# One w2 fetch moved up, weight sums spread over rounds, balancing in two parts, a sum of x in halves: attention and eight routed experts on one Trainium2 core

## The chip, the cores and the metric

The kernel runs on one core of one Trainium2 chip. The core has five engines that run side by side, each with its own queue of instructions that it works through strictly in order: TensorE (matmuls, PE in the profile; its weight loads are PEld), VectorE (DVE), ScalarE (ACT), GpSimd (POOL) and SyncE (SP). Engines wait for each other through semaphores. Matmuls write to PSUM, a small memory of eight banks of 128 x 512 float32 values, which VectorE and ScalarE empty into the larger SBUF. GpSimd's queue also issues the DMA transfers that bring in weights. The metric is the device time of one execution in microseconds, taken as the median of several runs; less is better.

## The reference

Attention over 4 x 8 heads with 768 positions of 64 features: an 8 x 8 matrix per head is balanced (five times exp, rows divided by their sums, columns divided by theirs) and mixes blocks of 96 keys and values before an ordinary softmax attention. Its output is x, 3072 tokens of 512 features, the input of eight experts:

```python
logits = x @ w_gate
logits = logits - logits.max()
P = np.exp(logits)
for _ in range(8):
    P /= P.sum(1, keepdims=True) + 1e-09
    P /= P.sum(0, keepdims=True) + 1e-09
    P *= N / E
for e in range(E):
    h = np.maximum(x @ w1[e], 0.0)
    ye = h @ w2[e]
    out += P[:, e:e + 1] * ye
```

Every token goes through every expert (512 to 1024 hidden features and back to 512), and the 3072 x 8 weights P come out of eight balancing iterations over the whole table.

## The kernel before

**Stages.** Up to about 125 us the kernel does the attention, batch by batch, with expert 0 for the tokens that are done between its matmuls. From there on it does the last tokens of expert 0 (the generator `last_dense`, lines 765 and 773), the eight balancing iterations (the generator `balance`), and experts 1 to 7.

**Experts 1 to 7** multiply in Strassen's way: seven products of quarter matrices instead of eight, paid for with sums. Four kinds of sums are needed: of w1 (`sum_w`, line 406, eight additions for an expert, GpSimd), of w2 (`sum_w2`, line 518, eight, GpSimd), of x (`sum_x`, line 528, four for each third of the tokens; one third on VectorE before the stage, one on GpSimd, and the last, `sum_x(2)`, on VectorE), and of the hidden values (`Pair.sums`, line 691, three on GpSimd for each pair of token tiles, into a tile `hs`; line 641 on GpSimd or line 644 on VectorE for one more, `s3`). Sums of w1 and the fourth sum of x are in place.

**Rounds.** The main loop runs over rounds r. A chunk n is one third of the tokens (p) of one expert (e) and takes four rounds (i = 0 to 3). In each round there are seven steps p1, p5, p6, p2, p7, p3, p4 (`hidden`, matmuls at line 590) of the chunk, and between them seven products q1 to q7 (line 701) of the pair k = r - 5, in the order q5, q7 of the pair before, q1, q4 of the pair before, q6, q2, q3. In the rounds 0 to 4 there is no pair yet, and what is left of `last_dense` stands between the steps. PSUM has a ring of five banks `bk` for the steps and of three banks `oacc` for the products; the third of these holds the balancing's table until round 5.

After p7 and p3 VectorE evicts a bank with line 579 (relu of a sum, into the hidden values hT); after p2 and p4 ScalarE does it with line 576. After a product VectorE adds the weighted result to the output (`gather`, line 651). q1 goes to the same bank as q5, and waits for the gather of q5.

**The order of the work** is written out by hand: every instruction of this stage is pinned, so each engine gets its instructions in the order in which the Python code calls them.

- GpSimd in a round: the load of w1 or w2 if one is due (lines 89 and 94), then the three sums of the pair of the next round, then `weights(n)`, which takes n sums from a queue of generators. A load is a DMA that GpSimd issues; the sums that read it wait for its landing on GpSimd, and with them all that is queued behind. Expert 2's w2 is loaded in round 8, and the queue gets its sums there; `weights` takes 4 in the rounds 5, 6 and 7, and then 1 or 2 in turn:

```python
weights((0, 2, 2, 0, 0)[r] if r < 5 else 4 if r < 8 else 1 + i % 2)
```

- The balancing generator is advanced by `next(chain)`: seven times between the steps of `last_dense`, by the letters C of a string, and in the rounds 0 to 4 after three of every four steps. An iteration has three parts: row sums and their reciprocals (lines 560 to 562, VectorE); the division by them and the column sums over the tiles (lines 564 and 565); then one small matmul over the partitions (line 567, TensorE), its reciprocal and the division (lines 568 to 571, VectorE). The matmul is in TensorE's queue like any other, and all that is behind it waits until VectorE's column sums are there.

- The four sums of `sum_x(2)` are advanced by the letters X of the same string (three), and the last of them, in place on xtT, at the end of round 6. Round 8 is the first to read it.

Of the kernel before, what the change touches and what calls it, by code (L numbers as in the profile page):

```python
# [17 lines left out]
ALU = mybir.AluOpType  # L18


def mkap(t, dims, off=0):
    return bass.AP(tensor=t.tensor, offset=t.offset + off, ap=dims)
# [3 lines left out]
def kernel(  # L26
# [14 lines left out]
    N, Dm, E, F = 3072, 512, 8, 1024  # L41
# [45 lines left out]
    def load_w1(e):  # L87
        w1t[e] = wp.tile([128, 4, F], BF16, name="w1e")
        pin(nc.gpsimd.dma_start(out=w1t[e],
                                in_=moe_w1[e].rearrange("(kk k) f -> k kk f", k=128)))  # L90

    def load_w2(e):
        w2t[e] = (wq if e else wcp).tile([128, 8, Dm], BF16, name="w2e")
        pin(nc.gpsimd.dma_start(out=w2t[e],
                                in_=moe_w2[e].rearrange("(fb k) f -> k fb f", k=128)))
# [302 lines left out]
    def sum_w(e):  # L398
        wct[e] = (wcq if e % 2 == 0 else wcp).tile([128, 3, 2, F // 2], BF16, name="wc")
        for kk in range(2):  # L400
            a11, a21 = (w1t[e][:, kk, f:f + 512] for f in (0, 512))
            a12, a22 = (w1t[e][:, 2 + kk, f:f + 512] for f in (0, 512))
            s1, s2, s4 = (wct[e][:, j, kk, :] for j in range(3))
            for a, b, o, c in ((a21, a22, ALU.add, s1), (s1, a11, ALU.subtract, s2),
                               (a11, a21, ALU.subtract, a21), (a12, s2, ALU.subtract, s4)):
                pin(nc.gpsimd.tensor_tensor(out=c, in0=a, in1=b, op=o))  # L406
                yield

    with tc.tile_pool(name="ps0", bufs=7, space=bass.MemoryType.PSUM,
# [37 lines left out]
        for h in range(0, 8, 2):  # L447
            nc.vector.tensor_tensor(
                out=Rt[0][:, h:h + 2],
                in0=mkap(pbps, [pbps.ap[0], [1, 2], [32, 8], [0, 16]], off=h),  # L450
                in1=mkap(mask16, [mask16.ap[0], [0, 2], [0, 8], [1, 16]]), op=ALU.mult)
# [71 lines left out]
    def sum_x(p, eng, hold=pin):  # L523
        ta, tb = (slice(1024 * p + 512 * i, 1024 * p + 512 * i + 512) for i in range(2))
        b11, b12, b21, b22 = (xtT[:, k:k + 2, t] for k in (0, 2) for t in (ta, tb))
        x1, x2, x4 = (xc[:, j, :, 512 * p:512 * p + 512] for j in range(3))
        for a, b, c in ((b12, b11, x1), (b22, x1, x2), (b21, x2, x4), (b22, b12, b12)):
            hold(eng.tensor_tensor(out=c, in0=a, in1=b, op=ALU.subtract))
            yield

    onesc = mpc.tile([128, 128], F32)
    nc.gpsimd.memset(onesc, 1.0)
# [2 lines left out]
    for _ in sum_x(0, nc.vector, lambda ins: ins):  # L535
        pass

    def balance():

        room = rings["oacc"][2]  # L540
        G = room[:, 0:NT * E].rearrange("p (t e) -> p t e", e=E)
        sums = room[:, 192:192 + NT]
        csps = room[:, 256:256 + E]
        gmps = room[:, 384:512]
        gm = mpc.tile([128, 1], F32)
        pin(nc.vector.reduce_max(out=gm, in_=glog.rearrange("p t e -> p (t e)"), axis=AX.X))
        pin(nc.tensor.matmul(gmps[0:1, :], gm, I128, start=True, stop=True))
        gm1 = mpc.tile([1, 1], F32)
        pin(nc.vector.reduce_max(out=gm1, in_=gmps[0:1, :], axis=AX.X, negate=True))
        yield  # L550
        pin(nc.tensor.matmul(csps[:, 0:1], onesc[0:1, :], gm1, start=True, stop=True))
        gneg = mpc.tile([128, 1], F32)
        pin(nc.vector.tensor_copy(gneg, csps[:, 0:1]))
        pin(nc.scalar.activation(out=G, in_=glog, func=AF.Exp, bias=gneg))
        rs2 = mpc.tile([128, NT], F32)
        cs2 = mpc.tile([128, E], F32)
        cs1 = mpc.tile([128, E], F32)
        yield
        for it in range(8):
            pin(nc.vector.reduce_sum(out=sums, in_=G, axis=AX.X))  # L560
            pin(nc.vector.tensor_scalar_add(rs2, sums, 1e-9))
            pin(nc.vector.reciprocal(out=rs2, in_=rs2))
            yield
            pin(nc.vector.tensor_mul(G, G, mkap(rs2, [rs2.ap[0], rs2.ap[1], [0, E]])))
            pin(nc.vector.reduce_sum(out=cs2, in_=G.rearrange("p t e -> p e t"), axis=AX.X))
            yield
            pin(nc.tensor.matmul(csps, onesc, cs2, start=True, stop=True))
            pin(nc.vector.tensor_scalar(out=cs1, in0=csps, scalar1=float(E) / N,
                                        scalar2=1e-9 * E / N, op0=ALU.mult, op1=ALU.add))
            pin(nc.vector.reciprocal(out=cs1, in_=cs1))  # L570
            pin(nc.vector.tensor_mul(glog if it == 7 else G, G,
                                     mkap(cs1, [cs1.ap[0], [0, NT], cs1.ap[1]])))
            yield
# [168 lines left out]
    def scale0(ts):  # L742
        for t in ts:
            pin(nc.scalar.activation(out=osbl[:, t, :], in_=osbl[:, t, :], func=AF.Copy,
                                     scale=glog[:, t, 0:1]))

    def last_dense():
# [7 lines left out]
        for c in range(2):  # L755
# [14 lines left out]
            for tt in range(3):  # L770
# [7 lines left out]
                yield  # L778

    dense, chain, xs = last_dense(), balance(), sum_x(2, nc.vector)  # L780
    for step in "TTCXTTCXTTCCXTTCCTTTCTT":
        next({"T": dense, "C": chain, "X": xs}[step])
    held_x = mpc.tile([128, 2], BF16)
    pin(nc.gpsimd.tensor_copy(held_x, xc[:, 2, 0, 1024:1026]))

    queue = [sum_w2(1), sum_x(1, nc.gpsimd)]

    def weights(n):
        while n and queue:
            if next(queue[0], 0) is None:  # L790
                n -= 1
            else:
                queue.pop(0)
# [7 lines left out]
    for m, o in enumerate(ends):  # L801
        e, p, hT, _ = chunks[-1]
# [4 lines left out]
    for r in range(len(pairs) + 6):  # L807
        n, i = r // 4, r % 4
        if n < C:
            e, p, hT, s3 = chunks[n]  # L810
            if i == 0 and (n == 1 or n > 1 and p == 0) and e + 1 < E:
                load_w1(e + 1)
                queue.append(sum_w(e + 1))
            if r == 8 or p == 1 and i == 2 and n > 1 and e + 1 < E:
                load_w2(2 if r == 8 else e + 1)
                queue.append(sum_w2(2 if r == 8 else e + 1))
            steps, rest = hidden(e, p, i, hT, s3, r < 4)
        else:
            steps, spares, rest = spares[:7], spares[7:], None
        k = r - 5  # L820
        if k + 1 in range(len(pairs)):
            pairs[k + 1].sums()
        weights((0, 2, 2, 0, 0)[r] if r < 5 else 4 if r < 8 else 1 + i % 2)
        now = pairs[k] if k in range(len(pairs)) else None
        if r < 5:
            outs = [lambda: next(dense), None, lambda: next(dense), None,
                    lambda: next(dense)]
        else:
            outs = [getattr(a, b) for a, b in
                    ((now, "q5"), (before, "q7"), (now, "q1"), (before, "q4"),  # L830
                     (now, "q6"), (now, "q2"), (now, "q3")) if a]
        if now and now.last:
            plains, steps = iter(steps), []
            outs = [next(plains) if o == "x" else getattr(before if o[1:] else now, "q" + o[0])
                    for o in "5 7' x 1 x 4' 6 x 2 x 7 x x 3 4".split()]
            now = None
        if r == 5:
            for _ in chain:
                pass
        for j in range(max(len(steps), len(outs))):  # L840
            if j < len(steps):
                steps[j]()
                if j == 3 and n < C:
                    if k + 1 in range(1, 12):
                        scale0([8 * ((k + 1) // 4) + (k + 1) % 4 + 4 * m for m in range(2)])
                    if k + 1 in range(len(pairs)):
                        pairs[k + 1].keep()
            if j < len(outs) and outs[j]:
                outs[j]()
            if r < 5 and j != 3 and (6 * r + j - (j > 3)) % 4 != 3:  # L850
                next(chain, 0)
            if r == 4 and j in (2, 5):
                scale0([4 if j == 2 else 0])
            if j == 1 and late:
                late()
                late = None
            if r == 6 and j == 6:
                next(xs)
        late, before = rest, now
        if n >= C and not spares and not before:  # L860
            break
# [30 lines left out]
```

## Time and profile before

| what | us |
|---|---|
| median of 3 runs | 669.74 (669.25 to 670.33) |
| the profiled execution | 669.11 |
| its span, first to last instruction | 667.3 |
| TensorE busy | 653.6 |
| VectorE busy | 475.2 |
| GpSimd busy | 470.8 |
| ScalarE busy | 386.3 |
| TensorE's granted clock | 1.00 throughout |

The profile comes from one execution. "Busy" is the time in which an engine had an instruction under way. A list of waits names an engine, the instruction that waited, and the one that released it, with the total in us, the number of times and the longest. A view in order of time gives the start in us, the duration of an instruction or of several alike in a row (xN), the engine, the line in the code, the operation, and output and inputs with their shapes; in brackets, when the engine stood idle before it, for how long and who released it. Matmuls overlap, so a group's duration reaches beyond the start of the next. GpSimd's starts and ends are rougher than those of the others.

### The profile page before, as it was taken

To read this page: it belongs to the slowest core of one execution; us is meant where nothing else is said; L and a number is where in the kernel's file an instruction comes from. 1 tells how busy PE (TensorE), PEld (TensorE's weight loads), DVE (VectorE), ACT (ScalarE), POOL (GpSimd) and SP (SyncE) were. 2 spreads that over 40 slices of the span, in tenths; PEclk is the share of its full clock that TensorE was granted. 3 is DMA by queue.
4 is the path that set the end of the run, shared out by engine and by line. 5 is a ranking of instruction groups with operands and counts; after the bars stand their busy time and mean duration, and the time that the engine had idled before them with its cause. 6 is when DMAs were issued, how large, how long until landed. Compare 5 with 4: busy or idle time off the path is not lost.

```text
span 667.3 us, 13145 instructions
## 1 busy us (share of the span) xinstructions
PE 653.6 (98%) x5051; PEld 423.8 (64%) x5051; DVE 475.2 (71%) x909; ACT 386.3 (58%) x757; POOL 470.8 (71%) x439
## 2 busy tenths in 40 slices
PE   5999999999999999999999999999999999999997
PEld 3565565544666666666666666666666666666665
DVE  6864667666767777777777777777777777777775
ACT  4777657467777756555645555555555555555540
POOL 3643650096969998779796979789687969936641
PEclk9999999999999999999999999999999999999999
DMA  9999934003042131030403040302203040000224
GB/s 151 176 221 152 186 70 64 1 1 63 1 64 36 30 44 22 5 60 1 63 1 64 1 64 1 55 10 29 36 0 64 1 65 1 1 1 33 95 81 173
DMA packets 33167, 36.52 MB, mean 55 GB/s; under 512 B 2064, under 2 KB 26224, under 8 KB 33104
## 3 DMA queue, kind: packets, MB, share of 16 engines
q0 software_dynamic: 26880, 27.69, 26.2%
q1 hardware_dynamic: 5712, 7.40, 3.6%
q8 instruction: 39, 0.64, 0.4%
q10 hardware_dynamic: 512, 0.59, 0.4%
q14 instruction: 24, 0.20, 0.1%
HBM read 52.45 MB, written 6.29 MB: 88 GB/s over the span
## 4 chain that ended last, share of the span: by engine, by line
PE 88%; POOL 4%; DMA 2%; ACT 2%; issue 1%; DVE 1%; ACTq 0%; POOLq 0%
PE oacc L701 35%; PE bk L590 34%; PE bank L363 4%; PE bank L376 4%; POOL hs L691 2%; DMA w2e<-in_moe_w_dram 1%; PE bank L217 1%; POOL wc L406 1%; PE bk L667 1%; PE bank L258 1%; PE unread L418 1%; DMA qt<-in_q_dram 1%; PE bk L765 1%; PE bank L240 1%; PE bank L194 1%
## 5 line engine op out<-in xcount | busy, mean ns | idle before, releaser
L651 DVE SCALAR_TENSOR_TENSOR osbl<-oacc,glog,osbl 128x256 f32<-128x256 f32 (+1 forms) x411 | 219.1, 534 | 126.3 <-PE oacc L701 116.9
L576 ACT ACTIVATE hT<-bk 128x512 bf16<-128x512 f32 (+1 forms) x176 | 104.4, 593 | 147.4 <-PE bk L590 127.9
L590 PE MATMUL bk<-xtT,w1e 128*128 128x512 bf16 x504 | 149.1, 379 | 0.0
L701 PEld LDWEIGHTS <-hs 128*128 128x128 bf16 x984 | 96.2, 98 | 63.9 <-POOL hs L691 1.2
L701 PEld LDWEIGHTS <-hT 128*128 128x128 bf16 x904 | 88.4, 98 | 58.3 <-issue 1.1
L691 POOL TENSOR_TENSOR hs<-hT 128x512 bf16<-128x512 bf16 x82 | 94.7, 1155 | 36.2 <-DVE hT L579 30.8
L701 PE MATMUL oacc<-w2e,hT 128*128 128x256 bf16 x764 | 114.6, 273 | 0.4 <-DVE osbl L651 0.3
L691 POOL TENSOR_TENSOR hs<-hs,hT 128x512 bf16<-128x512 bf16 x82 | 94.7, 1154 | 6.4
L590 PE MATMUL bk<-xc,wc 128*128 128x512 bf16 x336 | 99.1, 379 | 0.1
L691 POOL TENSOR_TENSOR hs<-hT,hs 128x512 bf16<-128x512 bf16 x82 | 94.6, 1153 | 6.4
L701 PE MATMUL oacc<-w2e,hs 128*128 128x256 bf16 x616 | 92.4, 273 | 0.0
L590 PEld LDWEIGHTS <-w1e 128*128 128x128 bf16 x672 | 65.8, 98 | 11.8 <-issue 0.3
L625 ACT COPY p<-bk 128x512 f32<-128x512 f32 x84 | 49.3, 587 | 25.8 <-PE bk L590 25.8
L579 DVE CUSTOM_DVE_ANT_0 hT<-bk,p 128x512 bf16<-128x512 f32 x84 | 58.1, 691 | 8.4 <-PE bk L590 3.1
L619 ACT COPY u<-bk 128x512 f32<-128x512 f32 x84 | 49.3, 587 | 22.1 <-PE bk L590 21.9
L610 ACT COPY bk<-bk 128x512 f32<-128x512 f32 x84 | 48.2, 574 | 20.4 <-PE bk L590 20.4
L579 DVE CUSTOM_DVE_ANT_0 hT<-bk,u 128x512 bf16<-128x512 f32 x84 | 57.1, 679 | 1.3 <-PE bk L590 0.8
L701 PE MATMUL oacc<-w2s,hs 128*128 128x256 bf16 x368 | 55.2, 273 | 0.7 <-POOL hs L691 0.7
L590 PEld LDWEIGHTS <-wc 128*128 128x128 bf16 x504 | 49.3, 98 | 8.0 <-issue 0.2
L644 DVE SCALAR_TENSOR_TENSOR s<-bk,hT 128x512 bf16<-128x512 f32 x80 | 54.4, 680 | 0.0
L590 PE MATMUL bk<-xtT,wc 128*128 128x512 bf16 x168 | 50.0, 379 | 0.0
L590 PE MATMUL bk<-xc,w1e 128*128 128x512 bf16 x168 | 50.0, 379 | 0.0
(138 smaller groups left out, 840.8 us busy)
## 6 DMA issues: line engine op xcount, KB each, us to landing
w2e<-in_moe_w_dram POOLq DMA_DIRECT2D x8, 1024.0 KB, 9.4
w1e<-in_moe_w_dram POOLq DMA_DIRECT2D x7, 1024.0 KB, 8.0
out_dram<-osbl SPq DMA_DIRECT2D x21, 256.0 KB, 2.0
vt<-in_v_dram POOLq DMA_DIRECT2D x3, 768.0 KB, 11.1
qt<-in_q_dram POOLq DMA_DIRECT2D x4, 384.0 KB, 10.0
kt<-in_k_dram POOLq DMA_DIRECT2D x4, 384.0 KB, 11.7
kt<-in_k_dram POOLq DMA_DIRECT2D x2, 768.0 KB, 14.5
qt<-in_q_dram POOLq DMA_DIRECT2D x2, 768.0 KB, 17.5
```

The source lines that it names most:

```text
L363: pin(nc.tensor.matmul(hps[:, 0:n], w1t[0][:, kk, fb * 128:(fb + 1) * 128], xtT[:, kk, c0:c0 + n], start=(kk == 0), stop=(kk == 3)))
L376: pin(nc.tensor.matmul(oacc, hTs[:, fb, tt * 128:(tt + 1) * 128], w2t[0][:, fb, :], start=(fb == 0), stop=(fb == 7)))
L576: relu = lambda o, x: nc.scalar.activation(out=o, in_=x, func=AF.Relu)
L579: return nc.vector._custom_dve(TENSOR_ADD_SAT, out=o, in0=x, in1=y, s0=TOP, s1=0.0)
L590: pin(nc.tensor.matmul(ps, wa[:, kk, :], xa[:, kk, :], start=(first and kk == 0), stop=(kk == 1), skip_group_check=True))
L610: pin(nc.scalar.copy(t["w"], t["u"]))
L619: pin(nc.scalar.copy(t["u2"], t["u"]))
L625: pin(nc.scalar.copy(t["p5"], t["v"]))
L644: pin(nc.vector.scalar_tensor_tensor(out=s3[:, i, :], in0=t["w"], scalar=0.0, in1=c12, op0=ALU.max, op1=ALU.subtract))
L651: pin(nc.vector.scalar_tensor_tensor(out=o, in0=ps, scalar=glog[:, t, e:e + 1], in1=o, op0=ALU.mult, op1=ALU.add))
L691: pin(nc.gpsimd.tensor_tensor(out=s[:, c], in0=a, in1=b, op=o))
L701: pin(nc.tensor.matmul(ps, h[:, fb, :], w[:, fb, :], start=(first and fb == 0), stop=(fb == 3), skip_group_check=True))
```

## The change

Four edits, all in the stage of the experts:

- Expert 2's w2 is loaded in round 5 instead of 8. Its sums still enter the queue in round 8. For the other experts load and sums stay where they were.
- `weights` takes 2 sums in each of the rounds 5 to 11, instead of 4 in the rounds 5 to 7 and 1 or 2 after.
- A balancing iteration has two parts instead of three: the stop between the row sums' reciprocals and the division is gone. The generator is advanced five times in the dense stretch instead of seven, and in the rounds 0 to 4 after two of every four steps instead of three.
- The last sum of `sum_x(2)` is made in two halves, of one 512-element row block each, at the ends of rounds 6 and 7.

```diff
@@ sum_x
         for a, b, c in ((b12, b11, x1), (b22, x1, x2), (b21, x2, x4), (b22, b12, b12)):
-            hold(eng.tensor_tensor(out=c, in0=a, in1=b, op=ALU.subtract))
-            yield
+            for k in ((slice(0, 1), slice(1, 2)) if p == 2 and c is b12 else (slice(0, 2),)):
+                hold(eng.tensor_tensor(out=c[:, k], in0=a[:, k], in1=b[:, k],
+                                       op=ALU.subtract))
+                yield
@@ balance
             pin(nc.vector.reciprocal(out=rs2, in_=rs2))
-            yield
             pin(nc.vector.tensor_mul(G, G, mkap(rs2, [rs2.ap[0], rs2.ap[1], [0, E]])))
@@
-    for step in "TTCXTTCXTTCCXTTCCTTTCTT":
+    for step in "TTCXTTCXTTCXTTCTTCTTT":
         next({"T": dense, "C": chain, "X": xs}[step])
@@ the rounds
+            if r == 5 or p == 1 and i == 2 and n > 1 and e + 1 < E:
+                load_w2(2 if r == 5 else e + 1)
             if r == 8 or p == 1 and i == 2 and n > 1 and e + 1 < E:
-                load_w2(2 if r == 8 else e + 1)
                 queue.append(sum_w2(2 if r == 8 else e + 1))
@@
-        weights((0, 2, 2, 0, 0)[r] if r < 5 else 4 if r < 8 else 1 + i % 2)
+        weights((0, 2, 2, 0, 0)[r] if r < 5 else 2 if r < 12 else 1 + i % 2)
@@
-            if r < 5 and j != 3 and (6 * r + j - (j > 3)) % 4 != 3:
+            if r < 5 and j != 3 and (6 * r + j - (j > 3)) % 4 < 2:
                 next(chain, 0)
@@
-            if r == 6 and j == 6:
+            if r in (6, 7) and j == 6:
                 next(xs)
```

## The prediction

> **What bounds the kernel now.** I read the shares first, then TensorE's waits, then the three engines' instructions in order of time from 140 to 210 us, because only there does TensorE stand still between 125 us and the last rounds. The page's first part:
>
> ```profile
> PE 653.6 (98%) x5051; PEld 423.8 (64%) x5051; DVE 475.2 (71%) x909; ACT 386.3 (58%) x757; POOL 470.8 (71%) x439
> ```
>
> TensorE is the bound; a change that leaves its work alone can win only its 13.7 us of idle time. Its waits (us in total, times, longest):
>
> ```profile
> PE bank L170 <- DMA qt<-in_q_dram: 7.1, 1, 7.1
> PE oacc L701 <- POOL hs L691: 0.7, 1, 0.7
> PE oacc L567 <- DVE cs L565: 0.5, 2, 0.3
> PE oacc L701 <- DVE osbl L651: 0.3, 1, 0.3
> ```
>
> The first is the start, which the change does not touch; the other four standstills are one for each part of the change. Their size I take from starts, since a group's duration contains the drain of its last matmul: in step, two matmuls of 512 columns or four of 256 start the next group 0.43 us later, four of 384 after 0.65, four of 512 after 0.86. TensorE in order of time (start, us, group):
>
> ```profile
> 147.15 0.81 PE L765 MATMUL oacc<-xtT,w1e 128*128 128x384 bf16 x4
> 148.29 0.39 PE L567 MATMUL oacc<-cs,onesc 128*128 128x8 f32 x2 [0.32 <-DVE cs L565]
> ...
> 158.75 1.03 PE L773 MATMUL oacc<-w2e,hs 128*128 128x512 bf16 x4
> 159.99 0.39 PE L567 MATMUL oacc<-cs,onesc 128*128 128x8 f32 x2 [0.21 <-DVE cs L565]
> ...
> 178.29 0.59 PE L590 MATMUL bk<-xc,wc 128*128 128x512 bf16 x2
> 179.14 0.60 PE L701 MATMUL oacc<-w2e,hT 128*128 128x256 bf16 x4 [0.25 <-DVE osbl L651]
> ...
> 195.20 0.59 PE L590 MATMUL bk<-xtT,w1e 128*128 128x512 bf16 x2
> 196.46 0.61 PE L701 MATMUL oacc<-w2s,hs 128*128 128x256 bf16 x4 [0.66 <-POOL hs L691]
> ```
>
> Late against the step: 148.29 by 0.49, 159.99 by 0.38, 179.14 by 0.42, 196.46 by 0.83. VectorE and GpSimd at the same places:
>
> ```profile
> 146.72 0.30 DVE L562 RECIPROCAL rs<-rs 128x24 f32<-128x24 f32 x1
> 146.95 0.63 DVE L579 CUSTOM_DVE_ANT_0 hT<-bk,u 128x512 bf16<-128x512 f32 x1
> 147.49 0.35 DVE L564 TENSOR_TENSOR oacc<-oacc,rs 128x192 f32<-128x192 f32 x1
> 147.88 0.36 DVE L565 TENSOR_REDUCE cs<-oacc 128x8 f32<-128x192 f32 x1
> ...
> 177.42 1.27 DVE L528 TENSOR_TENSOR xtT<-xtT 128x1024 bf16<-128x1024 bf16 x1
> 178.62 0.86 DVE L651 SCALAR_TENSOR_TENSOR osbl<-oacc,glog,osbl 128x256 f32<-128x256 f32 x2
> ```
>
> ```profile
> 178.10 1.60 POOL L406 TENSOR_TENSOR w1e<-w1e 128x512 bf16<-128x512 bf16 x1
> ...
> 194.14 1.15 POOL L518 TENSOR_TENSOR w2e<-w2e 128x512 bf16<-128x512 bf16 x1 [5.22 <-DMA w2e<-in_moe_w_dram]
> 195.25 1.15 POOL L691 TENSOR_TENSOR hs<-hT 128x512 bf16<-128x512 bf16 x1
> ```
>
> To be seen: the eviction L579 stands between the two halves of a balancing iteration and makes the column sum L565 late; a sum of x that takes 0.67 to 0.69 elsewhere takes 1.27 here and holds the gather L651; and GpSimd, having sent for w2 of expert 2 at 184.34, stands 5.22 us before the first sum that reads it, with the sums of a pair (L691) queued behind, for which TensorE waits.
>
> **The change part by part.** The listed order of the two programs gives TensorE, ScalarE and SyncE the same instructions in the same order. VectorE's order differs in three places, GpSimd's from 162 to 217 us.
>
> *Balancing in two parts.* Same instructions; eight fewer stops, five instead of seven taken in the dense stretch. In six of eight iterations nothing moves. In the fifth and the eighth, L579 now stands behind L564 and L565.
> Fifth: L564 starts 0.34 after L562 (as at 142.95 and 143.29), at 147.06; L565 at 147.46; its matmul 0.41 later (as 143.69 to 144.10), at 147.87. TensorE is there at 147.80. Gain 0.42. L579 runs from 147.8 to 148.4 instead of 147.0 to 147.6; its PSUM bank is next asked for two rounds later, and GpSimd's sum that reads its result starts at 150.62 anyway. L568 follows at 148.4 (148.71 before), so the next iteration has its matmul in time.
> Eighth, 0.42 earlier: L562 at 157.69, L564 158.03, L565 158.43, result usable at 158.84; TensorE arrives at 159.19 and does not wait. Gain 0.38, and 0.09 more since the group after L567 starts 0.15 us later where nothing waited (155.58 to 155.73) and 0.24 where it did: 0.47. The price: L579, the last eviction of the chunk, ends at 159.43 instead of 159.27, and GpSimd's sums of pair 0 start at 159.52 instead of 159.36, against a TensorE that is 0.89 ahead. They have their first result at 160.7 and q5 asks for it at 164.1: covered by 3.4 us. The stall at 144.10 (0.3) stays.
>
> *w2 sooner, sums spread.* Pace first. Three sums of a pair take 3.58 from start to start (172.17 to 175.75), four of w1 4.57, two thus 2.28. Before, a round asks 3.58 + 4.57 = 8.15 of GpSimd while TensorE needs 6.08; after, 5.86. Walking GpSimd on from 159.52: pair 0 to 163.08; L641, 1.11, to 164.19; the w2 issue, 0.95 with its gap (184.34 to 185.29), to 165.14; pair 1 to 168.71; two w1 sums to 171.06; pair 2 to 174.64; two to 176.86; pair 3 to about 180.6; two to 183.0; pair 4 to 186.6; two to 188.9; then pair 5. The issue stands ahead of pair 1 and costs it 0.95; its first sum is ready at 166.3 and wanted at 170.0. Pair 4 is ready at 184.3, wanted at 188.2; pair 5, which was late, at 190.1 against 194.3. The transfer runs from 164.2 for 9.7 us to 174, after that of w1 (sent for at 154.21; the DMA share is 0.82 up to 163 us, 0.01 in the next five), and its first reader is due at 188.9 or later, behind pair 5 in round 9. In rounds 9 to 11 two sums of w2 stand for two of w1; 5.9 per round still fits 6.08, and from round 13 the order is that of before. Gain: the whole 0.83.
>
> *The last sum of x in halves.* It moves from one place (177.42, at the end of round 6) to the ends of rounds 6 and 7. What the place bears: q1 at 178.72 needs the gather of q5 (0.48, handed over in 0.04), which may start at 178.20, 0.78 after the sum was asked for; the whole sum held VectorE 1.20. A half is not in the trace. From below it is half of 0.67, from above the 1.27 of the whole. By slope, as a gather of 256 columns takes 0.481 and one of 512 0.750, I take 0.40. The wait comes on top: 0.60 above normal here, while GpSimd finished an operation of 176.99 to 178.15 and stretched its next from 1.15 to 1.60. From the walk: asked for at 176.53 with GpSimd's sum ending near 176.9, so (less the 0.13 by which 0.60 is under 0.73) a wait of 0.24, and VectorE is free after 0.57 of its 0.78. The second: asked for at 182.60, GpSimd's sum ending at 183.0, wait 0.29, free after 0.62. Neither holds TensorE; each has some 0.2 to spare. Gain 0.42, with ends of 0.42 and, both halves meeting a sum just begun (1.02 + 0.40 - 0.07 = 1.35, less 0.78: 0.57 each), minus 0.72. The values rest on the walk, so I take the upper end and keep the lower for the range. The second half is read first in round 8 at 185.2; it is there at 183.5.
> The Trainium skill, SBUF — State Buffer, "Who interferes with whom", says that a VectorE instruction with two SBUF inputs and a GpSimd instruction that reads SBUF exclude each other for a whole instruction, and the second to come is fully blocked. The 1.27 and 1.60 agree with that; by that rule two instructions can be blocked twice, which speaks against cutting the sum. With that in its worst phase at both places the sum below would be 1.00 in place of 2.14.
>
> Sum: 0.42 + 0.47 + 0.83 + 0.42 = 2.14 us. The profiled execution took 669.11 us, 1.81 around its span of 667.3; it becomes 666.97 (span 665.2). The median of the runs is 0.63 above it and would become 667.60. I say **667.5**, the median's value moved a little towards that of the profiled execution.
>
> **Rivals.**
> *The halves collide.* GpSimd's phase is good to perhaps 0.2 us and so is the margin. One half in the worst phase costs 0.57, both 1.14: saved 1.57 or 1.00, from the median 668.2 or 668.7. For it: GpSimd is busy without a gap there. Against: the two walked waits.
> *The stall at 196 stays.* If GpSimd's sums became longer beside other neighbours, pairs would be late again in rounds 9 to 11: 2.14 less 0.83 is 1.31, 668.4. The point is the lead of 3.7 to 4.2 us; against it: 82 triples average 1.15 an operation.
> *The early issue holds GpSimd (slower).* One w2 issue waited 7.39 us for its buffer at 97.7. If the one for expert 2, in its new place at 164.2, found its buffer taken, all pair sums stand behind it. It decides when the hold passes the 3.7 us of pair 1; above 7.2 us the gain and 1.34 more are lost. At 7.39: 7.39 - 3.7 - 2.14 = 1.55, 671.3. Against it: the buffer is the second of two and the attention that used the memory ended by 126 us; the issue now names waits on old transfers of that stage, which it did not before, and they are long done.
>
> **How the numbers follow.** This kernel's measurement tells apart about 0.2%, 1.34 us: below 668.4 is faster, above 671.1 slower. As forecast, or within 0.3 us of it: 0.70. Halves collide: 0.15, faster with one, on the edge with both. Stall stays: 0.06, on the edge. Early issue holds: 0.04, slower. Unseen: 0.05, mostly slower or nothing. Faster 0.77, same 0.16, slower 0.07. The range goes from 666.5 (own time's result less half a microsecond of spread) to 668.9 (both halves collide, with 0.2 of spread).
>
> **What would show it.** In TensorE's waits of the changed kernel the three lines below the first are gone, or L567 alone stays with under 0.1; GpSimd has no wait on w2e near 190 us; L579 stands behind L565 at 148 and 159 us; two sums of x of 0.5 to 0.8 us with POOL neighbours of 1.2 to 1.5. Wrong it would be if a half took over 1.0 us with TensorE idle behind it, or if idle time before L701 came up between 165 and 215 us for L691.

## The result, and the profile after

| | before | changed | ratio |
|---|---|---|---|
| median, first chip, 6 runs each | 669.34 us | 666.83 us | 0.9960 (0.9947 to 0.9973) |
| median, second chip, 22 and 6 runs | 669.03 us | 666.87 us | 0.9971 (0.9960 to 0.9982) |
| profiled execution | 669.11 us | 666.23 us | |
| its span | 667.3 us | 664.5 us | |

The changed kernel is faster by 2.5 us on one chip and 2.2 us on another, 0.3 to 0.4%. Forecast were 2.14 us and 667.5 us. Ratios, here and below, are taken over the executions within 1.5% of the fastest of their kernel.

The first part of the changed kernel's page, TensorE's line:

```profile
PE 651.7 (98%) x5051; PEld 423.3 (64%) x5051; DVE 475.9 (72%) x910; ACT 385.6 (58%) x757; POOL 470.7 (71%) x439
```

All of TensorE's waits in the changed kernel (us in total, times, longest):

```profile
PE bank L170 <- DMA qt<-in_q_dram: 6.8, 3, 6.4
PE bank L444 <- DVE Prep L439: 0.8, 1, 0.8
PE bank L217 <- DVE kTs L200: 0.3, 1, 0.3
PE bank L194 <- DMA kt<-in_k_dram: 0.3, 1, 0.3
```

The three waits on L567, L651 and L691 of before are gone. What is left in this list lies in the attention, which the change does not touch. The four places, in TensorE's order of time (lines have moved: L568 is now the balancing's matmul, L566 the column sum, L580 the eviction, L529 the sum of x, L652 the gather, L692 the pair sums and L702 a product):

```profile
146.53 0.81 PE L766 MATMUL oacc<-xtT,w1e 128*128 128x384 bf16 x4
147.26 0.39 PE L568 MATMUL oacc<-cs,onesc 128*128 128x8 f32 x2
...
157.72 1.03 PE L774 MATMUL oacc<-w2e,hs 128*128 128x512 bf16 x4
158.59 0.28 PE L568 MATMUL oacc<-cs,onesc 128*128 128x8 f32 x2
...
176.79 0.59 PE L591 MATMUL bk<-xc,wc 128*128 128x512 bf16 x2
177.22 0.60 PE L702 MATMUL oacc<-w2e,hT 128*128 128x256 bf16 x4
...
193.28 0.59 PE L591 MATMUL bk<-xtT,w1e 128*128 128x512 bf16 x2
193.72 0.60 PE L702 MATMUL oacc<-w2s,hs 128*128 128x256 bf16 x4
```

From start to start these are 0.73 after a group that takes 0.65, 0.87 after one of 0.86, and 0.43 and 0.44 after groups of 0.43: late by 0.08, 0.01, 0 and 0.01 us, where before it was 0.49, 0.38, 0.42 and 0.83. VectorE and GpSimd at these places, in order of time:

```profile
146.84 0.36 DVE L566 TENSOR_REDUCE cs<-oacc 128x8 f32<-128x192 f32 x1
147.12 0.68 DVE L580 CUSTOM_DVE_ANT_0 hT<-bk,u 128x512 bf16<-128x512 f32 x1
...
175.92 0.64 DVE L529 TENSOR_TENSOR xtT<-xtT 128x512 bf16<-128x512 bf16 x1
176.48 0.99 DVE L652 SCALAR_TENSOR_TENSOR osbl<-oacc,glog,osbl 128x256 f32<-128x256 f32 x2
...
182.00 0.66 DVE L529 TENSOR_TENSOR xtT<-xtT 128x512 bf16<-128x512 bf16 x1
```

```profile
163.53 0.93 POOL L94 DMA_DIRECT2D w2e<-in_moe_w_dram  x1
...
175.12 1.16 POOL L406 TENSOR_TENSOR wc<-w1e,wc 128x512 bf16<-128x512 bf16 x1
176.23 1.34 POOL L692 TENSOR_TENSOR hs<-hT 128x512 bf16<-128x512 bf16 x1
...
190.78 1.15 POOL L692 TENSOR_TENSOR hs<-hT,hs 128x512 bf16<-128x512 bf16 x1
191.90 2.39 POOL L518 TENSOR_TENSOR w2e<-w2e 128x512 bf16<-128x512 bf16 x2
```

The eviction L580 now stands behind the column sum L566; the two halves take 0.64 and 0.66; GpSimd asks for w2 at 163.53 and goes from sum to sum at 191.9 without a wait.

**Where the time came from.** The stage that the change touches I measure from the first matmul of the last dense stretch (L765 before, L766 after) to the start of the last group of four at L667 (L668): 125.20 to 661.99, 536.79 us before, and 124.57 to 659.04, 534.47 us after: 2.32 less. The four places give 0.41 + 0.47 + 0.42 + 0.83 = 2.13 (the second counts the 0.10 by which the group after L568 follows sooner). Two late starts of 0.12 and 0.10 near 292 and 487 us, there before and not after, bring it to 2.35. The remaining 0.56 us between the two profiled executions (2.88 less 2.32) is the earlier first matmul, 124.57 instead of 125.20, less some 0.08 behind the stage. Ahead of it the instructions are the same, and in the profiles at full clock of the runs below this start lies anywhere between 125.4 and 127.5 us. It is the spread of the attention stage, and so the stage lengths tell more than the times where a few tenths count.

### The profile page after: what moved, and what is told of

Read it like the earlier page. It is cut to its first block, busy times and chain, and to the rows that moved or that the text cites. A ratio compares the mean times of both kernels' runs of the same rounds, so it can differ in the third digit from the quotient of the medians.

```text
span 664.5 us, 13146 instructions
## 1 busy us (share of the span) xinstructions
PE 651.7 (98%) x5051; PEld 423.3 (64%) x5051; DVE 475.9 (72%) x910; ACT 385.6 (58%) x757; POOL 470.7 (71%) x439
## 4 chain that ended last, share of the span: by engine, by line
PE 92%; DVE 3%; DMA 3%; ACT 2%; issue 0%; ACTq 0%
PE bk L591 38%; PE oacc L702 38%; PE bank L376 4%; PE bank L363 3%; DMA qt<-in_q_dram 2%; PE oacc L774 1%; PE bk L668 1%; PE bank L217 1%; PE bk L766 1%; PE bank L258 1%; PE bank L194 1%; DVE kTs L200 1%; PE oacc L766 1%; PE bk L774 1%; PE bank L240 1%; PE bank L146 0%
## 5 line engine op out<-in xcount | busy, mean ns | idle before, releaser
L652 DVE SCALAR_TENSOR_TENSOR osbl<-oacc,glog,osbl 128x256 f32<-128x256 f32 (+1 forms) x411 | 219.4, 535 | 124.8 <-PE oacc L702 115.6
L702 PEld LDWEIGHTS <-hs 128*128 128x128 bf16 x984 | 96.3, 98 | 63.0 <-issue 0.3
L702 PEld LDWEIGHTS <-hT 128*128 128x128 bf16 x904 | 88.4, 98 | 57.9 <-issue 0.6
L692 POOL TENSOR_TENSOR hs<-hT 128x512 bf16<-128x512 bf16 x82 | 95.1, 1159 | 39.5 <-DVE hT L580 34.0
L702 PE MATMUL oacc<-w2e,hT 128*128 128x256 bf16 x764 | 114.6, 273 | 0.1
L692 POOL TENSOR_TENSOR hs<-hs,hT 128x512 bf16<-128x512 bf16 x82 | 94.6, 1154 | 6.4
L692 POOL TENSOR_TENSOR hs<-hT,hs 128x512 bf16<-128x512 bf16 x82 | 94.6, 1153 | 6.4
L702 PE MATMUL oacc<-w2e,hs 128*128 128x256 bf16 x616 | 92.4, 273 | 0.0
L580 DVE CUSTOM_DVE_ANT_0 hT<-bk,p 128x512 bf16<-128x512 f32 x84 | 58.1, 692 | 7.7 <-PE bk L591 3.1
L580 DVE CUSTOM_DVE_ANT_0 hT<-bk,u 128x512 bf16<-128x512 f32 x84 | 57.2, 681 | 1.6 <-PE bk L591 0.6
L702 PE MATMUL oacc<-w2s,hs 128*128 128x256 bf16 x368 | 55.2, 273 | 0.0
```

The costliest lines, as they stand in the source:

```text
L580: return nc.vector._custom_dve(TENSOR_ADD_SAT, out=o, in0=x, in1=y, s0=TOP, s1=0.0)
L652: pin(nc.vector.scalar_tensor_tensor(out=o, in0=ps, scalar=glog[:, t, e:e + 1], in1=o, op0=ALU.mult, op1=ALU.add))
L692: pin(nc.gpsimd.tensor_tensor(out=s[:, c], in0=a, in1=b, op=o))
L702: pin(nc.tensor.matmul(ps, h[:, fb, :], w[:, fb, :], start=(first and fb == 0), stop=(fb == 3), skip_group_check=True))
```

## The experiments

Theory: each part removes its own stall, the stalls are exact sums over the neighbours, and the sum of x is held by GpSimd instruction by instruction. Rivals: one part alone did all of it, the parts undo each other, or the two engines share a port's bandwidth instead of excluding each other. The lengths below are those of the stage as just defined; 536.79 is before, 534.47 the changed kernel. Where no ratio is given, the kernel was executed once, for its profile.

### The balancing alone

```diff
             pin(nc.vector.reciprocal(out=rs2, in_=rs2))
-            yield
-    for step in "TTCXTTCXTTCCXTTCCTTTCTT":
+    for step in "TTCXTTCXTTCXTTCTTCTTT":
-            if r < 5 and j != 3 and (6 * r + j - (j > 3)) % 4 != 3:
+            if r < 5 and j != 3 and (6 * r + j - (j > 3)) % 4 < 2:
```

> Only the two-part balancing is put into the kernel before. If each gain stands at its own place and the places add up: the L567 matmul near 148 us is late by under 0.1 us instead of 0.49 and the one near 160 us by nothing instead of 0.38, together 0.9 us; the stalls near 179 us (0.42, sum of x) and 196 us (0.83, w2) stay, within 0.1 for the second and within 0.4 for the first, whose size hangs on GpSimd's phase. Time 0.9 us less than before. Rival, the later eviction L579 makes the pair sums late: then the 0.9 comes back as idle time before L701 between 164 and 180 us, and the time is that of before.

Ratio 0.9989 (0.9971 to 1.0008): no measurable gain (medians 668.36 and 669.12 us). The two matmuls were late by 0.07 and 0, as expected, and between 164 and 180 us no stall on the pair sums came up, so the rival is out; but at 196 us there was far more than 0.83. GpSimd and TensorE there, in order of time (L700 is a product here):

```profile
185.03 0.93 POOL L94 DMA_DIRECT2D w2e<-in_moe_w_dram  x1
...
196.15 1.15 POOL L518 TENSOR_TENSOR w2e<-w2e 128x512 bf16<-128x512 bf16 x1 [6.52 <-DMA w2e<-in_moe_w_dram]
```

```profile
194.78 0.59 PE L589 MATMUL bk<-xtT,w1e 128*128 128x512 bf16 x2
198.46 1.04 PE L700 MATMUL oacc<-w2s,hs 128*128 128x256 bf16 x4 [3.09 <-POOL hs L690]
```

TensorE was due at 195.21 and came 3.25 later. Two things add up: w2 landed 11.12 us after its issue (9.80 before), and the issue came only 10.18 us ahead of TensorE's need (184.34 to 195.63, 11.29, before). This execution was not a typical one: it took 672.40 us, the other nine 668.04 to 668.64. The second of the two is the interesting one, so I took a second profile of the same kernel:

> The two-part balancing alone, a second profile. GpSimd's sums of pair 0 start with the last eviction of chunk 0, which did not come sooner, while TensorE is 0.9 us ahead; so the fetch of w2, issued behind those sums, is as late as before and the stall at 196 us grows from 0.83 by what TensorE has gained, 1.1 us with the smaller loss at 179 us, to some 1.9 us with the usual 9.7 us of landing: the gain of this part alone is given back. In the first profile it was 3.25, with a landing of 11.1 us. Rival, the late landing alone made it: with 9.7 us the stall is about 0.8 again.

```profile
185.49 0.93 POOL L94 DMA_DIRECT2D w2e<-in_moe_w_dram  x1
...
194.40 1.15 POOL L518 TENSOR_TENSOR w2e<-w2e 128x512 bf16<-128x512 bf16 x1 [4.31 <-DMA w2e<-in_moe_w_dram]
```

```profile
195.23 0.59 PE L589 MATMUL bk<-xtT,w1e 128*128 128x512 bf16 x2
196.71 0.61 PE L700 MATMUL oacc<-w2s,hs 128*128 128x256 bf16 x4 [0.89 <-POOL hs L690]
```

Late by 1.05 here, with a landing of 8.91, the shortest seen. All these figures follow one sum: from landing to the product it is 2.32 us (a sum of w2, the first pair sum), so TensorE is late by landing + 2.32 - lead: 9.80 + 2.32 - 11.29 = 0.83 before, 11.12 + 2.32 - 10.18 = 3.26 and 8.91 + 2.32 - 10.17 = 1.06 here. The lead had indeed shrunk by 1.1 us in both profiles, since GpSimd's chain starts with the last eviction of chunk 0, which does not come sooner when TensorE does. With the landing of 9.80 the stall would be 1.95, as expected; the rival, that the late landing alone made it, fails, since the shortest landing still gave more than 0.83. So this part by itself mostly moves its gain to the wait on w2. The stage of the second profile is 535.95, 0.84 less than before; but with a landing of 8.91 the kernel before would by the same sum have had no stall there and a stage of 535.96. This rests on two profiles and the sum: the interval of the times, which reaches from 0.3% faster to 0.1% slower, does not decide it.

### w2 sooner and sums spread, alone

```diff
+            if r == 5 or p == 1 and i == 2 and n > 1 and e + 1 < E:
+                load_w2(2 if r == 5 else e + 1)
             if r == 8 or p == 1 and i == 2 and n > 1 and e + 1 < E:
-                load_w2(2 if r == 8 else e + 1)
-        weights((0, 2, 2, 0, 0)[r] if r < 5 else 4 if r < 8 else 1 + i % 2)
+        weights((0, 2, 2, 0, 0)[r] if r < 5 else 2 if r < 12 else 1 + i % 2)
```

> Only the earlier fetch of w2 and the spread sums are put into the kernel before. Places add up: no wait of GpSimd on w2e near 190 us, the stall of 0.83 at 196 us is gone, the two L567 stalls (0.49, 0.38) stay. By the port lock, the whole sum of x near 177.4 us now meets a GpSimd sum that ends near 177.9: wait 0.3, 0.98 us long instead of 1.27, TensorE late by 0.13 instead of 0.42. Time 0.8 to 1.1 us less. Rival, the sum of x has a fixed slowed length beside GpSimd: it stays at 1.27 and TensorE 0.42 late.

Ratio 0.9992 (0.9975 to 1.0010), which does not resolve a gain of this size; stage 535.70, 1.09 less. The wait on w2 is gone and nothing is late at 196 us; the two L567 matmuls are late by 0.49 and 0.37 as before. VectorE, in order of time:

```profile
179.70 0.97 DVE L528 TENSOR_TENSOR xtT<-xtT 128x1024 bf16<-128x1024 bf16 x1
180.60 0.86 DVE L651 SCALAR_TENSOR_TENSOR osbl<-oacc,glog,osbl 128x256 f32<-128x256 f32 x2
```

The uncut sum takes 0.97 instead of 1.27 and TensorE is late by 0.12, against 0.98 and 0.13 expected. A fixed slowed length is out: only GpSimd's place in time has changed. The sum of the places, 0.83 + 0.30 = 1.13, is the 1.09 of the stage.

### Either half of that part

```diff
+            if r == 5 or p == 1 and i == 2 and n > 1 and e + 1 < E:
+                load_w2(2 if r == 5 else e + 1)
             if r == 8 or p == 1 and i == 2 and n > 1 and e + 1 < E:
-                load_w2(2 if r == 8 else e + 1)
```

> The kernel before with w2 of expert 2 fetched in round 5, the sums at the old pace of 4, 4, 4. By GpSimd's walk: nothing waits for w2 near 190 us, pair 5 is ready about 5 us sooner than before, the stall of 0.83 at 196 us is gone; pair 3, 0.95 us later by the issue, is ready at 182.9 for 183.5 and costs nothing or a few tenths. Rival, the pace is what counts: pair sums stay late and idle time before L701 comes up near 184 or 196 us.

```diff
-        weights((0, 2, 2, 0, 0)[r] if r < 5 else 4 if r < 8 else 1 + i % 2)
+        weights((0, 2, 2, 0, 0)[r] if r < 5 else 2 if r < 12 else 1 + i % 2)
```

> The kernel before with two sums in each of the rounds 5 to 11 and w2 still fetched in round 8. By GpSimd's walk: the issue comes at 182 to 183 us, lands at about 192 to 193, and its first sum is due at 193, behind pair 5 and no longer ahead of it; so the stall of 0.83 is gone here as well, and either edit alone would do. Rival, the early fetch is needed: GpSimd waits for w2e by 2 us or more and TensorE is late at 196 us or one round later.

Neither has a late product at 196 us; TensorE there with the earlier fetch alone, then with the spread alone:

```profile
195.91 0.59 PE L590 MATMUL bk<-xtT,w1e 128*128 128x512 bf16 x2
196.34 0.60 PE L701 MATMUL oacc<-w2s,hs 128*128 128x256 bf16 x4
```

```profile
195.84 0.59 PE L590 MATMUL bk<-xtT,w1e 128*128 128x512 bf16 x2
196.27 0.60 PE L701 MATMUL oacc<-w2s,hs 128*128 128x256 bf16 x4
```

The stages are 535.71 and 535.98 us. The 0.27 between them is the uncut sum of x: it leaves TensorE 0.15 late with the earlier fetch, whose issue shifts GpSimd's sums, and 0.42, as before, with the spread alone. The spread alone in GpSimd's order of time:

```profile
182.63 0.93 POOL L94 DMA_DIRECT2D w2e<-in_moe_w_dram  x1
...
191.87 1.16 POOL L691 TENSOR_TENSOR hs<-hT,hs 128x512 bf16<-128x512 bf16 x1
192.98 2.39 POOL L518 TENSOR_TENSOR w2e<-w2e 128x512 bf16<-128x512 bf16 x2
```

With fewer sums ahead of it the fetch is issued 1.7 us sooner (2.3 against the start of the stage), and its first reader stands at 192.98, 10.35 us after the issue and behind pair 5 instead of ahead of it. With a landing of 11.1 GpSimd would wait there for 0.8 us, but the pair behind it, whose sums begin at 195.33, is first wanted at 202.35, so by these rows TensorE would not. With both edits the fetch has 28 us (163.53 to 191.90). Either edit alone was enough for this stall.

### The halves alone, the whole in the changed kernel, both halves in one place

```diff
-            hold(eng.tensor_tensor(out=c, in0=a, in1=b, op=ALU.subtract))
-            yield
+            for k in ((slice(0, 1), slice(1, 2)) if p == 2 and c is b12 else (slice(0, 2),)):
+                hold(eng.tensor_tensor(out=c[:, k], in0=a[:, k], in1=b[:, k], op=ALU.subtract))
+                yield
-            if r == 6 and j == 6:
+            if r in (6, 7) and j == 6:
```

> Only the two halves are put into the kernel before. Lock: the first half is asked for at 177.4 us with 0.6 to wait, takes 0.6 + 0.41 = 1.0 us and leaves TensorE 0.15 late instead of 0.42; the second waits some 0.35 and leaves nothing. Gain 0.27. Sharing of bandwidth instead of a lock: each half takes half of 1.27, 0.64, and the whole 0.42 is gone. The stalls at 148, 160 and 196 us stay at 0.49, 0.38 and 0.83, the last within 0.3 since GpSimd is held up less.

The first half took the wait that the lock predicts:

```profile
177.77 1.00 DVE L529 TENSOR_TENSOR xtT<-xtT 128x512 bf16<-128x512 bf16 x1
...
184.00 0.76 DVE L529 TENSOR_TENSOR xtT<-xtT 128x512 bf16<-128x512 bf16 x1
```

TensorE was late by 0.15 behind the first and by nothing behind the second. The late start at 196 us was 0.17: w2 was read 9.15 us after its issue at 184.41, and the sum above gives 9.15 + 2.32 - 11.30 = 0.17. The stage is 535.69, 1.10 less than before: 0.27 here, 0.66 at 196 us, and the 0.2 of the two late starts near 292 and 487 us, which are gone here too. For the opposite, the same diff is taken out of the changed kernel:

> The changed kernel with the last sum of x in one piece again. Lock: GpSimd's phase at that place is that of the changed kernel, where the half waited 0.23 us; the whole takes 0.23 + 0.68 = 0.91 us and TensorE is late by 0.05 to 0.1. The cut itself would then be worth next to nothing here, and the 0.42 came from GpSimd's new phase. Rival, the cut is what removed the stall: it is back at 0.3 to 0.45.

```profile
178.85 0.91 DVE L528 TENSOR_TENSOR xtT<-xtT 128x1024 bf16<-128x1024 bf16 x1
```

```profile
179.72 0.59 PE L589 MATMUL bk<-xc,wc 128*128 128x512 bf16 x2
180.20 0.60 PE L700 MATMUL oacc<-w2e,hT 128*128 128x256 bf16 x4
```

0.91 us, and the product is late by 0.05. The stage is 534.72; the 0.25 over the changed kernel are this 0.05 and the two late starts near 292 and 487 us, which are here again. So in the changed kernel the cut itself is worth 0.05 us at its place, and 0.25 in the whole stage: the 0.42 went because GpSimd's instructions now end sooner after VectorE's request. The last of the three puts both halves at the end of round 6:

```diff
-            if r in (6, 7) and j == 6:
+            if r == 6 and j == 6:
                 next(xs)
+                next(xs)
```

> The changed kernel with both halves of the last sum of x behind each other at the end of round 6. Lock for a whole instruction: GpSimd takes the port between them, the first half takes 0.64 us as in the changed kernel and the second 1.3 to 1.4, and TensorE is late by about 1.1 us near 177 us. Sharing: two times 0.64, TensorE late by 0.36.

```profile
177.62 1.93 DVE L529 TENSOR_TENSOR xtT<-xtT 128x512 bf16<-128x512 bf16 x2
```

```profile
178.49 0.59 PE L591 MATMUL bk<-xc,wc 128*128 128x512 bf16 x2
180.00 0.60 PE L702 MATMUL oacc<-w2e,hT 128*128 128x256 bf16 x4 [0.92 <-DVE osbl L652]
```

Late by 1.08 (1.51 from start to start, less 0.43), stage 535.55, 1.08 more than the changed kernel. Sharing, which would give 0.36, is out. Cut in two at one place, the same sum costs more than uncut: GpSimd gets its next instruction in between, and the second half waits it out.

### The changed kernel again, and three tries to better it

The changed kernel without an edit:

> The changed kernel once more, beside the next two on one chip. If its gain is the sum of the four places (0.41 + 0.47 + 0.42 + 0.83 = 2.13 us) and the rest of what was first measured is the varying length of the stage ahead of 125 us, the time is 2.1 us under that of before (ratio 0.9968), and from the first matmul of the last dense stretch to the end there are 534.5 us as in its first profile. Rival, the change also shortens what lies ahead: 2.5 to 2.8 us less, and that stretch stays while the start comes 0.6 us sooner again.

666.87 us, ratio 0.9971 (0.9960 to 0.9982), stage 534.48 after 534.47 in its first profile. The start lies at 125.36 this time, so the early start of the first profile was chance. First try, on top of the changed kernel:

```diff
-            if r < 5 and j != 3 and (6 * r + j - (j > 3)) % 4 < 2:
-                next(chain, 0)
+            step = 6 * r + j - (j > 3)
+            if r < 5 and j != 3:
+                for _ in range(step in (0, 1, 4, 5) if step < 8 else 2 * (step % 4 == 1)):
+                    next(chain, 0)
-            outs = [getattr(a, b) for a, b in
+            outs = [getattr(a, b) if a else None for a, b in
-                     (now, "q6"), (now, "q2"), (now, "q3")) if a]
+                     (now, "q6"), (now, "q2"), (now, "q3")) if a or r == 5]
```

> The changed kernel with two more edits. From the fourth iteration on, the balancing's matmul stands one step later and the next iteration's VectorE part is called directly behind it: the 0.28 + 0.11 lost at 143.5 us and the 0.08 + 0.10 at 147.3 should go, 0.5 us. In round 5 the products keep the places that they have in every other round, with free steps between: of the 0.75 lost there between 163.5 and 168.5 us the last three pieces, 0.17 + 0.18 + 0.18, should go, and the first, 0.22, stay. Time 1.0 us under that of the changed kernel, some 3.4 under that of before, a ratio of 0.995. Rival, the waits move one step on: L568 or L702 stay late by the same sum at other places, and the time is that of the changed kernel.

Ratio 0.9976 (0.9967 to 0.9985), stage 534.83: not better. The products of round 5 did what was expected (0.22 + 0.05 left), the balancing did not:

```profile
148.63 0.39 PE L568 MATMUL oacc<-cs,onesc 128*128 128x8 f32 x2 [0.25 <-DVE cs L566]
...
152.28 0.59 PE L591 MATMUL bk<-xc,w1e 128*128 128x512 bf16 x2 [0.22 <-DVE hT L580]
```

0.57 of late starts became 1.21: I had reckoned four steps between two matmuls as equally long, but dense work stands only in the first half of a round, and the distance from the matmul at 145.71 to the next one's turn at 148.2 was 0.4 short for VectorE's part; then an eviction behind a whole iteration held p4. Second try, the round 5 products alone:

```diff
-            outs = [getattr(a, b) for a, b in
+            outs = [getattr(a, b) if a else None for a, b in
-                     (now, "q6"), (now, "q2"), (now, "q3")) if a]
+                     (now, "q6"), (now, "q2"), (now, "q3")) if a or r == 5]
```

> The changed kernel, with only the products of round 5 kept at the places that they have in every other round. Of 0.75 us lost in that round 0.48 go (in the run with two edits the same place kept 0.22 + 0.05); the balancing stays as in the changed kernel, without the 0.7 that its other placing cost there. Stage from the first matmul of the last dense stretch to the end 534.0 us instead of 534.5; time 0.5 under the changed kernel, ratio to before 0.996. Rival, the later products of round 5 make the gathers late for round 6: the 0.5 comes back there.

667.22 us, ratio 0.9976 (0.9966 to 0.9986), stage 534.48, that of the changed kernel. The 0.48 was won in round 5 and lost again. VectorE's first half there:

```profile
177.46 1.09 DVE L529 TENSOR_TENSOR xtT<-xtT 128x512 bf16<-128x512 bf16 x1
```

TensorE, and with it VectorE's request, came sooner, while GpSimd's chain did not; the half waits 0.68 instead of 0.23 and TensorE is 0.24 late at 179 us. With the two late starts of 0.10 and 0.12, which this version has again, that is the whole gain. Third try, on top of the second:

```diff
-            if r == 4 and j in (2, 5):
+            if r == 4 and j in (2, 6):
```

> The kernel of the run with the spaced products, with one scaling of an output tile on ScalarE (0.74 us, line 745) moved in round 4 behind the eviction of p4, which it delays. The 0.22 left at the second product step of round 5 shrinks to under 0.1 if that eviction is what p5 waits for. Rival, the scaling then delays the copy for p2 or p6 by as much, and the loss moves one or two steps on.

Ratio 0.9976 (0.9967 to 0.9985), no better. The execution that was profiled took 759.34 us with TensorE's granted clock at 0.85 throughout, so whether the 0.22 moved was not seen. No version tried is faster than the changed kernel.

## Why the prediction was right or wrong

The total was right: 2.14 us forecast, 2.2 and 2.5 measured, 2.32 in the stage. The median of 666.83 lies 0.67 under the 667.5, of which 0.40 is the base: 669.74 was the median of three executions, six gave 669.34. The walk through the engines held to a few hundredths: GpSimd's sums of pair 1, behind the issue of w2, were put at 165.14 and came at 164.49, which is 165.12 when the 0.63 of the earlier start is added; those of pair 5 were put at 188.9 and came at 188.31, which is 188.94.

- *Balancing, fifth and eighth iteration.* 0.42 and 0.47 forecast, 0.41 and 0.47 found; the matmul at 147 us stays 0.08 late (0.07 said), the stall one iteration earlier stays (0.28). The mechanism was right. Not said was that this gain hangs on the w2 part: without it, a TensorE that comes sooner shortens the lead of the fetch by the same amount.
- *w2 and the spread.* The 0.83 is gone, as said. The step took two edits where each was enough, and it took 0.83 as a fixed cost. The runs show that it is landing - 8.97 us in the kernel before, with landings from 8.9 to 11.1: between nothing and 2.15 us. That it was 0.83 in the profile read was chance. The early fetch takes away this spread as well.
- *The sum of x.* "Gain 0.42" was right and its cause half wrong. The halves' 0.64 and 0.66 agree with the 0.24 + 0.40 and 0.29 + 0.40 foretold. But the same walk, had I carried it through for the uncut sum, gives 0.24 + 0.67 - 0.07 = 0.84 against the 0.78 that the place bears, and so 0.06 of late start. The cut was credited with what GpSimd's new phase did: uncut it is late by 0.05. That the term of 0.42 came out was luck in part: the stall went, for another reason than the one given.
- *The rivals.* The colliding halves were a real danger: 0.24 in the spaced version, 1.08 with both in one place. In the last sums of x of the profiles at full clock VectorE waited for the GpSimd instruction then under way: each sum took what was left of that instruction when it was asked for (0.28 to 0.82 us) less 0.13, and then 0.67 for a whole or 0.41 for a half, to within 0.02. GpSimd's next was lengthened, by 0.06 to 0.20 behind a half and 0.32 to 0.45 behind a whole. The rule of the Trainium skill (SBUF — State Buffer, "Who interferes with whom") that was weighed against the change agrees with this. The stall at 196 did not stay; the early issue found its buffer free.
- *Not in the sum, and left open.* The late starts of 0.10 to 0.12 near 292 and 487 us. TensorE waits there for VectorE's eviction after p7, which begins 0.40 to 0.42 us after VectorE's gather ahead of it has ended (291.37 to 291.79 before), though p7's matmuls were done at 291.27; in the changed kernel it is 0.06 (288.61 to 288.67). This is so in all seven profiles with the last sum of x in one piece, in none of the four with halves and the products of round 5 as they were (the halves alone, both profiles of the changed kernel, both halves together), and again in the two with halves that move those products. Why VectorE starts late there no run tells.

## What to carry to other kernels

An engine's order decides which stall is paid; in a kernel with one full engine, list every place where it starts late, find the instruction just ahead of the one that it waits for, and move what need not stand there. Gains at such places are not independent: a chain on another engine that does not move with the first one turns a gain upstream into a later wait, so first take away the waits whose lead is short (a fetch with 28 us of lead instead of 11, or its first reader behind what is urgent instead of ahead of it), then the others. And where two engines exclude each other by whole instructions, as VectorE's sum of x and GpSimd's sums did here, the length of one of them is a matter of phase: the whole at a good place cost 0.05 us, two halves behind each other 1.08.

## What the runs showed of the hardware

In the first profile of the balancing alone, TensorE's standstill of 3.1 us cost more than itself. Stretches of that profile (from, to, length; busy us of PE, PEld, DVE, ACT, POOL; granted clock; DMA share; GB/s):

```profile
190.00:195.00 5.00, 5.00 (x37) 3.42 (x35) 3.59 (x8) 3.72 (x7) 0.00 (x0) 1.00 0.74 119
...
198.40:199.40 1.00, 0.94 (x5) 0.69 (x6) 0.00 (x0) 0.00 (x0) 0.92 (x2) 0.50 0.00 0
199.40:200.40 1.00, 0.78 (x4) 0.39 (x4) 0.48 (x1) 0.01 (x1) 0.92 (x2) 0.50 0.00 0
200.40:201.40 1.00, 1.00 (x6) 0.66 (x5) 0.16 (x1) 0.57 (x1) 1.00 (x2) 0.63 0.00 0
201.40:203.00 1.60, 1.60 (x13) 1.07 (x11) 0.92 (x2) 1.29 (x3) 1.60 (x2) 1.00 0.00 0
```

The last matmul before it ended at 195.37. In finer stretches the granted clock is 1.00 from 195.40 to 197.70, 0.50 from 197.75 to 201.10, and 1.00 from 201.20: it fell during the standstill, 2.4 us after the last matmul, and was full again within 3 us of the restart. The four groups from 198.46 to 201.50 took 3.04 us instead of 1.74, 1.3 more. With this the stage of that profile adds up: 536.79, less 1.09 ahead of 196 us, plus 3.25 - 0.83 and 1.3, is 539.42, and 539.42 it was. After the standstill of 0.92 us in the version with both halves together the clock stayed at 1.00. So in this one profile a late transfer that let TensorE rest for some 3 us was paid almost half as much again. The Trainium skill (TensorE: Matmul & The Clock Gate, Part 1) tells of a gate to half rate after an idle window of about 3.4 us. The step to 0.50 here is of that kind, but 2.4 us without a matmul were enough for it.
